# Stated order on ScalarE and VectorE from the router on, in an attention and two-layer mixture kernel on one core

## Chip, cores and metric

The kernel runs on one core of a Trainium2 chip. The metric is the device time of one execution in microseconds (us); the time before is the median of three runs.

## What is computed

The reference takes q, k, v (4 batches, 12 heads, 448 positions, head size 64), applies attention with a soft cap, and feeds the result (1792 tokens of 768 values) through a dense two-layer part and then through eight experts that are chosen greedily by logit, each with room for 224 tokens.

```python
x = _attn_ref(q, k, v, cap)
h = np.maximum(x @ w_in, 0.0); x = (h * h) @ w_out
logits = x @ w_gate
order = np.argsort(-logits.flatten())
...
out[mask] = np.maximum(x[mask] @ w1[e], 0.0) @ w2[e]
```

## The kernel before, in words

The work goes batch by batch (four batches of 448 tokens). `attention` and the dense part (`hidden`, `output`) of different batches are interleaved by `merge`. Most operands are split into a high and a low part, so that one product is three matmuls; the first layer of experts 0 to 3 is done in plain fp32 (`PLAIN`).

The change concerns what follows, `second` (line 137). It states, in one stream, the second layer of the dense part for the last two batches and then the experts (`experts`, line 179), and beside it the side streams: the logits, the eight routes (`route`, line 612) and their lists (`listed`, line 739). A planner clock `te` counts the TensorE time that has been stated; a side stream is taken up again when `te` has reached the time it asked for. The waits that side streams ask for are constants, for each of them one for the dense part and one for the experts: START (7.7, 8.0) from a route's preparation to its first mask matmul, MASK (1.85, 3.4), VOTE (1.0, 2.6), REST (0.86, 2.2), LIST (6.0, 10.0) from a list's operations to its matmul (L761).

A route finds the expert that fills up next, by six passes over digits of six bits: VectorE writes a mask (L640), TensorE multiplies it (L676), VectorE makes votes of that (L681 to L684), TensorE adds them up (L687), VectorE sets the digit (L690). Behind the passes come tm (L696), three small matmul steps, A and V (L716 to L719), the count matmul (L722), and then on VectorE, with no yield between them, sn, slot, n, room, base, fu, es, todo and ei (L723 to L735) and at once the next route's preparation: lim, L, m, sg, key, D0, digit, mask, eo, mx, B, need, di, dig (L618 to L665). The list of the route is a stream of its own that begins 0.5 later: off, half, rel, r, tk, oh (L747 to L757). The last route (number 7) has no passes.

An expert's first layer makes eight tiles of 128 features (L867 plain, L874 split) in PSUM tiles named acc, of which there are two; for expert 0, tiles 2 to 5 lie in tiles named big. `evict` empties one: ScalarE's Relu (L884), then VectorE's low part (L885), both under `high_priority(5000)`; the side streams run under `high_priority(2000)`. The second layer is L913. In its second half the next expert's rows are transposed (L802) through the same acc tiles and copied by ScalarE (L807, or L809 with VectorE's low part L810 from expert 4 on).

Expert weights are loaded by SyncE twelve tiles ahead (L834) and split four tiles ahead of use (`split_weights`: ScalarE's cast L361, VectorE's subtraction L362). A plain tile is not split.

What sets the order of the work: the framework compiles each engine's instructions into one in-order queue. Engines under `manual_schedule` keep stated order; the others are ordered at compile time by a simulated timeline and the priorities. Before the change only TensorE is manual. `issue_after(x)` puts an ordering edge behind x on x's own engine.

Of the kernel before, what the change touches and what calls it, by code (L numbers as in the profile page):

```python
# [16 lines left out]
OP = mybir.AluOpType  # L17
# [14 lines left out]
NF2 = F2 // 128  # L32
OB = 4
TC = N // 128
# [7 lines left out]
NS = 128  # L42
# [43 lines left out]
class Kernel:  # L86
# [5 lines left out]
    def run(self):  # L92
        tc = self.tc
        PS = bass.MemoryType.PSUM
        with tc.tile_pool(name="keep", bufs=1) as self.keep, \
                tc.tile_pool(name="wts", bufs=1) as self.wts, \
                tc.tile_pool(name="psum", bufs=2, space=PS) as self.psum, \
                tc.tile_pool(name="dram", bufs=1, space=bass.MemoryType.DRAM) as self.dram, \
                ExitStack() as right, ExitStack() as left:
            self.setup()  # L100
            self.mp = right.enter_context(tc.tile_pool(name="moe1", bufs=1, side="right"))
            self.gpool = self.mp
            xs = right.enter_context(ExitStack())
            self.xp = xs.enter_context(tc.tile_pool(name="x", bufs=ND, side="right"))
            with tc.tile_pool(name="x32", bufs=ND, side="right") as self.xq:
                with tc.tile_pool(name="rows", bufs=ND + 1, side="right") as self.tp, \
                        tc.tile_pool(name="attn", bufs=2, side="right") as self.ap:
                    merge([(self.attention(0), 44.0)])
                    self.split_rows(0)
                    merge([(self.hidden(0), 58.0), (self.attention(1), 44.0)])  # L110
                    for b in range(2, NB):
                        self.split_rows(b - 1)
                        streams = [(chain(self.output(b - 2), self.hidden(b - 1)), 118.0), (self.attention(b), 44.0)]
                        if b == NB - 1:
                            streams.append((self.gate_decode(), 30.0))
                        with tc.manual_schedule(engines={mybir.EngineType.PE}):
                            merge(streams)
                self.split_rows(NB - 1)
            self.gp = left.enter_context(tc.tile_pool(name="gate", bufs=1))
            last = left.enter_context(ExitStack())  # L120
            self.gpool = last.enter_context(tc.tile_pool(name="last", bufs=1))
            with tc.tile_pool(name="gate_load", bufs=3, side="right") as self.gl:
                with tc.manual_schedule(engines={mybir.EngineType.PE}):
                    merge([(self.hidden(NB - 1), 60.0), (self.gate_weights(), 80.0)])
            xs.close()
            self.tp = right.enter_context(tc.tile_pool(name="rows2", bufs=2, side="right"))
            self.rp = right.enter_context(tc.tile_pool(name="route", bufs=1, side="right"))
            self.router_setup()

            def room():  # L130
                last.close()
                self.ep = left.enter_context(tc.tile_pool(name="expert", bufs=2))

            with tc.manual_schedule(engines={mybir.EngineType.PE}):
                self.second(room)

    def second(self, room):
# [601 lines left out]
    def listed(self, k, es):  # L739

        nc, v = self.nc, self.nc.vector

        def T(shape, dt, name, bufs=1):
            return self.rp.tile(shape, dt, name=name, bufs=bufs)

        off, rel = T([128, 1], F32, "off"), T([128, TC], F32, "rel")
        v.tensor_scalar(off, es, float(CAP), float(CAP * NE + 1), op0=OP.mult, op1=OP.subtract)  # L747
        half, tk = T([128, TC, 2], BF, "half"), T([128, TC, 2, 2], BF, "tk")
        v.tensor_scalar(half[:, :, 0], self.slot, off, float(TP), op0=OP.add, op1=OP.is_lt)
        v.tensor_scalar(half[:, :, 1], self.slot, off, float(TP), op0=OP.add, op1=OP.is_ge)  # L750
        v.tensor_scalar(rel, self.slot, off, None, op0=OP.add)
        r = T([128, TC], BF, "r")
        v.scalar_tensor_tensor(r, half[:, :, 1], -float(TP), rel, op0=OP.mult, op1=OP.add)
        v.tensor_tensor(tk, self.tok[:, :, None, :].to_broadcast([128, TC, 2, 2]),
                        half[:, :, :, None].to_broadcast([128, TC, 2, 2]), op=OP.mult)
        oh = T([128, NS, TC], BF, "oh")
        self.picks = v.tensor_tensor(oh, self.slots, r[:, None, :].to_broadcast([128, NS, TC]), op=OP.is_equal)  # L757
        yield LIST[self.late], 0.0
        pi = self.psum.tile([128, 2, 2], F32, name="aux")
        for c in range(TC):  # L760
            nc.tensor.matmul(pi.rearrange("p a b -> p (a b)"), oh[:, :, c],  # L761
                             tk[:, c].rearrange("p a b -> p (a b)"), start=(c == 0), stop=(c == TC - 1))
        ix = T([TP, 2], F32, "ix")
        v.tensor_copy(ix, pi[:TP, :, 1])
        rows, idx = [], []
        for h in range(2):
            i = T([TP, 1], I32, f"idx{h}", 8)
            v.scalar_tensor_tensor(i, pi[:TP, h, 0:1], 128.0, ix[:, h:h + 1], op0=OP.mult, op1=OP.add)
            idx.append(i)
        while self.stored < DA or k > self.fed + 1 or k > self.gathered:  # L770
            yield 1.0, 0.0
        self.rows[k] = [self.gather(0, idx), None, idx]
        while self.stored < ND:
            yield 1.0, 0.0
        self.rows[k][1] = self.gather(1, idx)
        yield GATHER[k > 0], 0.8
        self.gathered = k + 1
# [65 lines left out]

    def split_expert(self):
        if len(self.ew[self.eready]) > 1:
            with self.tc.issue_after(self.picks.ins) if self.eready < 2 * NF2 else nullcontext():
                self.ew[self.eready] = self.split_weights(*self.ew[self.eready])

    def expert(self, k):
        nc, ep = self.nc, self.ep  # L850
# [83 lines left out]
def merge(streams):  # L934
    live = [[g, 0.0, total] for g, total in streams]
    while live:
        s = min(live, key=lambda x: x[1] / x[2])
        try:
            s[1] += next(s[0])
        except StopIteration:  # L940
            live.remove(s)
# [46 lines left out]
```

## Time and profile before

| | us |
|---|---|
| median of three runs (1072.57 to 1076.85) | 1075.96 |
| the profiled execution | 1073.57 |
| its span, first to last instruction | 1071.8 |
| PE busy | 1035.0 |
| DVE (VectorE) busy | 604.4 |
| ACT (ScalarE) busy | 470.8 |

The mean granted clock of TensorE is 0.991. The router's stage begins near 583 us, where the first matmuls of L562 stand, the first expert's matmuls near 749 us. Matmul records overlap, since they are pipelined; the step from start to start is what counts.

### The profile page before, as it was taken

Reading aid. Unit: us, or ns where it says so; the run is one execution under the profiler, and the core shown is the slowest. Engines: PE = TensorE matmul, PEld = TensorE weight load, DVE = VectorE, ACT = ScalarE, POOL = GpSimd, SP = SyncE. Lnnn points to the kernel's source line nnn. Section 1 sums busy time; section 2 is a strip of 40 time slices with the busy share of each in tenths; the row PEclk is TensorE's granted clock in tenths of the full one; section 3 lists DMA queues with packets and bytes.
Section 4 is the critical chain, followed back from the end, with each engine's and each line's share of the span. In section 5 each row is a group of like instructions: output and inputs, shape, how many; then the busy total and the mean of one; then the engine's idle time right before and its main releaser. Section 6 shows DMA issues by size and latency. Waiting matters only on the chain. (4 is left out here: it accounts for less than half of the span.)

```text
span 1071.8 us, 15662 instructions
## 1 busy us (share of the span) xinstructions
PE 1035.0 (97%) x5690; PEld 819.6 (76%) x5690; DVE 604.4 (56%) x1148; ACT 470.8 (44%) x725; POOL 245.8 (23%) x181
## 2 busy tenths in 40 slices
PE   6889999999999999999999999998999999999996
PEld 2235655777677777777887888887899998989996
DVE  5997999997222165556311244453656455676550
ACT  5867686544564633464543100012232232544551
POOL 0217785764221322221000100002220201021000
PEclk9999999999999999999999999998999999999999
DMA  8644777799655489978885368666673447556620
GB/s 284 240 149 139 253 274 255 243 323 339 228 176 185 164 293 343 367 274 283 294 297 173 126 195 283 194 203 199 209 273 144 134 164 274 187 189 208 212 72 27
DMA packets 102495, 237.60 MB, mean 222 GB/s; under 512 B 11089, under 2 KB 21873, under 8 KB 102417
## 3 DMA queue, kind: packets, MB, share of 16 engines
q1 hardware_dynamic: 87776, 219.65, 59.8%
q0 software_dynamic: 3424, 11.19, 3.4%
q10 hardware_dynamic: 11216, 5.75, 2.0%
q8 instruction: 45, 0.74, 0.3%
q14 instruction: 34, 0.27, 0.1%
HBM read 194.08 MB, written 42.47 MB: 221 GB/s over the span
## 5 line engine op out<-in xcount | busy, mean ns | idle before, releaser
L461 PE MATMUL acc<-g,wh 128*128 128x448 f32 x384 | 150.4, 392 | 0.0
L404 PE MATMUL acc<-xh,wh 128*128 128x448 f32 x384 | 146.4, 383 | 0.8 <-ACT r L411 0.8
L405 PE MATMUL acc<-xl,wh 128*128 128x448 f32 x384 | 140.7, 367 | 0.9 <-DVE xl L321 0.9
L462 PE MATMUL acc<-g,wh 128*128 128x448 f32 x384 | 140.9, 367 | 0.0
L463 PE MATMUL acc<-g,wl 128*128 128x448 f32 x384 | 140.3, 365 | 0.0
L406 PE MATMUL acc<-xh,wl 128*128 128x448 f32 x384 | 139.5, 363 | 0.0
L913 PE MATMUL big<-wh,g 128*112 128x384 f32 x512 | 119.3, 343 | 0.6 <-DVE g L885 0.6
L243 ACT ACTIVATE p<-big,isc 128x896 f32<-128x896 f32 x96 | 85.8, 907 | 43.5 <-PE big L239 43.5
L272 DVE RECIPROCAL z<-z 128x448 f32<-128x448 f32 x24 | 70.8, 2949 | 58.0 <-ACT z L271 58.0
L416 DVE TENSOR_TENSOR g<-r,g 128x448 fp32r<-128x448 f32 x58 | 42.7, 737 | 104.0 <-ACT g L415 103.7
L404 PEld LDWEIGHTS acc<-xh,wh 128*128 128x128 f32 x384 | 71.8, 188 | 34.7 <-issue 16.3
L783 POOL DMA_INDIRECT xg<-x,idx x32 | 31.5, 986 | 286.3 <-PE aux L676 129.4
L244 ACT ACTIVATE p<-p,capt 128x896 f32<-128x896 f32 x96 | 89.3, 948 | 1.7
L913 PEld LDWEIGHTS big<-wh,g 128*112 128x112 f32 x512 | 86.3, 176 | 1.6 <-DVE g L885 1.0
L461 PEld LDWEIGHTS acc<-g,wh 128*128 128x128 f32 x384 | 73.8, 192 | 11.8 <-issue 5.6
L263 PE MATMUL aux<-p,v 128*64 128x448 f32 x384 | 81.4, 550 | 0.3 <-DVE z L271 0.3
L239 PE MATMUL big<-qk 64*128 64x448 f32 x288 | 73.3, 599 | 7.1 <-DMA qk<-qk 6.4
L405 PEld LDWEIGHTS acc<-xl,wh 128*128 128x128 f32 x384 | 72.1, 188 | 10.4 <-issue 3.5
L361 ACT CAST wh<-wf 128x768 fp32r<-128x768 f32 (+1 forms) x64 | 47.9, 751 | 70.2 <-DMA wf<-w 13.9
L411 ACT ACTIVATE r<-acc 128x448 f32<-128x448 f32 x64 | 34.7, 543 | 99.1 <-PE acc L406 87.6
L462 PEld LDWEIGHTS acc<-g,wh 128*128 128x128 f32 x384 | 73.0, 190 | 6.3 <-issue 2.2
L463 PEld LDWEIGHTS acc<-g,wl 128*128 128x128 f32 x384 | 72.5, 189 | 6.8 <-issue 0.7
(179 smaller groups left out, 1838.2 us busy)
## 6 DMA issues: line engine op xcount, KB each, us to landing
g<-w SPq DMA_DIRECT2D x62, 384.0 KB
wh<-wih SPq DMA_DIRECT2D x48, 384.0 KB
wl<-wil SPq DMA_DIRECT2D x48, 384.0 KB
wh<-woh SPq DMA_DIRECT2D x72, 256.0 KB
wl<-wol SPq DMA_DIRECT2D x72, 256.0 KB
wf<-w SPq DMA_DIRECT2D x33, 384.0 KB
raw<-w SPq DMA_DIRECT2D x33, 384.0 KB
raw<-w_in SPq DMA_DIRECT2D x16, 768.0 KB
```

Source lines behind the costliest of these rows:

```text
L239: nc.tensor.matmul(ps[:, s, :S], k[rows], q[rows], start=True, stop=True)
L243: nc.scalar.activation(p, ps[:, :n, :S], AF.Tanh, scale=self.isc)
L244: e = nc.scalar.activation(p, p, AF.Exp, scale=self.capt)
L263: nc.tensor.matmul(U[hp][s * 64:s * 64 + 64], vt[hp][:, c, s * 64:s * 64 + 64], P[hp, c][:, s if c < KB else 0], start=(c == 0), stop=(c = ...
L272: nc.vector.reciprocal(d, d)
L404: nc.tensor.matmul(ps, wh[:, d], xh, start=(d == 0), stop=False)
L405: nc.tensor.matmul(ps, wh[:, d], xl, start=False, stop=False)
L406: nc.tensor.matmul(ps, wl[:, d], xh, start=False, stop=(d == ND - 1))
L461: nc.tensor.matmul(ps, a, gh, start=(f == 0), stop=False)
L462: nc.tensor.matmul(ps, a, gl, start=False, stop=False)
L463: nc.tensor.matmul(ps, z, gh, start=False, stop=(f == NF - 1))
L913: nc.tensor.matmul(acc[h][:, s, :DM // 2], l, r[:, s * (DM // 2):(s + 1) * (DM // 2)], start=(j == 0 and first), stop=(j == NF2 - 1 and last))
```

## The change

ScalarE and VectorE join TensorE in the manual schedule around `second`. The ordering edge that held the splits of the first expert behind the latest list's oh is dropped, and with it the attribute that named it.

```diff
-            with tc.manual_schedule(engines={mybir.EngineType.PE}):
+            with tc.manual_schedule(engines={mybir.EngineType.PE, mybir.EngineType.Activation, mybir.EngineType.DVE}):
                 self.second(room)
...
         oh = T([128, NS, TC], BF, "oh")
-        self.picks = v.tensor_tensor(oh, self.slots, r[:, None, :].to_broadcast([128, NS, TC]), op=OP.is_equal)
+        v.tensor_tensor(oh, self.slots, r[:, None, :].to_broadcast([128, NS, TC]), op=OP.is_equal)
...
     def split_expert(self):
         if len(self.ew[self.eready]) > 1:
-            with self.tc.issue_after(self.picks.ins) if self.eready < 2 * NF2 else nullcontext():
-                self.ew[self.eready] = self.split_weights(*self.ew[self.eready])
+            self.ew[self.eready] = self.split_weights(*self.ew[self.eready])
```

## Rows read from the trace of the kernel before

**Rows 1.** Waits of PE from 583 us: waited for, us in total, times, longest.
```profile
PE aux L687 <- DVE votes L684: 4.3, 3, 3.6
PE acc L867 <- DVE g L885: 2.4, 1, 2.4
PE acc L874 <- DVE g L885: 2.0, 4, 1.3
...
PE big L913 <- DVE g L885: 0.6, 2, 0.4
```

**Rows 2.** Two stretches: busy us of PE, PEld, DVE, ACT, POOL, then PEclk, DMA, GB/s.
```profile
742.20:749.10 6.90, 6.15 (x27) 5.32 (x27) 2.12 (x9) 2.35 (x4) 1.16 (x2) 0.51 0.00 1
...
885.60:889.00 3.40, 3.19 (x9) 2.91 (x10) 3.40 (x11) 1.12 (x3) 0.00 (x0) 0.50 0.02 8
```

**Rows 3.** Timelines of ACT and DVE near 740 us: start, us, what [idle before].
```profile
739.60 0.83 ACT L361 CAST wh<-g 128x768 fp32r<-128x768 f32 x1 [6.55 <-DMA g<-w]
...
740.47 0.96 DVE L362 TENSOR_TENSOR wl<-g,wh 128x768 fp32r<-128x768 f32 x1 [4.28 <-ACT wh L361]
```

**Rows 4.** Timeline of PE in the first layers of experts 5 and 7.
```profile
962.81 0.28 PE L874 MATMUL acc<-xs,wl 128*128 128x224 f32 x1
964.38 0.48 PE L874 MATMUL acc<-xs,wh 128*128 128x224 f32 x2 [1.29 <-DVE g L885]
...
1037.89 0.27 PE L874 MATMUL acc<-xs,wl 128*128 128x224 f32 x1
1038.27 0.48 PE L874 MATMUL acc<-xs,wh 128*128 128x224 f32 x2
```

**Rows 5.** Timeline of DVE around the end of route 1.
```profile
676.33 0.39 DVE L716 TENSOR_TENSOR A<-aux,room 128x224 bf16<-128x224 f32 x1 [1.10 <-PE aux L709]
...
677.67 0.39 DVE L726 TENSOR_REDUCE n<-aux 128x8 f32<-128x224 f32 x1
677.98 0.38 DVE L723 TENSOR_REDUCE sn<-V 128x14 f32<-128x224 f32 x1
...
680.85 1.07 DVE L757 TENSOR_TENSOR oh<-slots,r 128x1792 bf16<-128x1792 bf16 x1
...
683.33 0.26 DVE L636 TENSOR_TENSOR B<-eo,mx 128x112 bf16<-128x112 f32 x1
```

**Rows 6.** Timeline of DVE at the end of route 7.
```profile
964.24 0.38 DVE L726 TENSOR_REDUCE n<-aux 128x8 f32<-128x224 f32 x1
964.65 0.17 DVE L727 TENSOR_TENSOR room<-room,n 128x8 f32<-128x8 f32 x1
964.74 0.16 DVE L728 TENSOR_TENSOR base<-base,n 128x8 f32<-128x8 f32 x1
```

**Rows 7.** Timelines of DVE and PE: A of route 0, list matmuls of routes 0 and 1.
```profile
640.02 0.39 DVE L716 TENSOR_TENSOR A<-aux,room 128x224 bf16<-128x224 f32 x1 [0.46 <-PE aux L709]
...
648.48 0.66 PE L761 MATMUL aux<-tk,oh 128*128 128x4 bf16 x8
...
683.99 0.95 PE L761 MATMUL aux<-tk,oh 128*128 128x4 bf16 x14
```

**Rows 8.** Timelines of DVE and PE in the first layer of expert 0.
```profile
758.70 0.39 DVE L716 TENSOR_TENSOR A<-aux,room 128x224 bf16<-128x224 f32 x1 [2.15 <-issue]
...
766.87 2.43 PE L867 MATMUL acc<-xs,g 128*128 128x224 f32 x12
```

**Rows 9.** Timelines of DVE and PE in the first layer of expert 3.
```profile
876.91 0.39 DVE L885 SCALAR_TENSOR_TENSOR g<-acc,g 128x224 fp32r<-128x224 f32 x1 [1.09 <-ACT g L884]
...
880.97 2.43 PE L867 MATMUL acc<-xs,raw 128*128 128x224 f32 x12
```

**Rows 10.** Timeline of PE in the second layer of expert 4.
```profile
941.97 0.27 PE L722 MATMUL aux<-A,unit 128*128 128x224 bf16 x1
...
948.24 0.60 PE L802 MATMUL acc<-cf,xg 112*128 112x112 f32 x4
```

**Rows 11.** Instructions of L810: duration in ns min/median/max, first and last start.
```profile
L810 DVE TENSOR_TENSOR xs<-acc,xs x12: 615/618/625, 909.7 to 1024.9; 128x448 fp32r<-128x448 f32 x12
```

## The prediction

> **What bounds the kernel now.** I read the waits of TensorE first, over the stretch from the router on (583 us to the end) [rows 1]. TensorE waits for little there, and nearly all of it is for VectorE: votes that come late, and evictions (tile g, line 885) that come late. Every other engine matters only through those waits. Second, the clock [rows 2]: behind the two longest of them (3.6 and 2.4 us) the granted clock is 0.51 and 0.50, that is 1.2 instead of 2.4 GHz, once from 742.20 to 749.10 and once from 885.60 to 889.00; over matmuls that ran there the loss is about half: 3.1 and 1.6 us. Third, why the votes were late [rows 3]: the compile-time order had put a weight split ahead of them. ScalarE's cast waited 6.55 us for its load, VectorE's subtraction waited 4.28 us for that cast, and the router's three small operations stood behind it.
>
> So the stage's recoverable loss can be summed. Gaps: 4.1 (of the 4.3 for votes; one gap of 0.2 is of another kind), 2.4, 2.0 and 0.6 us, together 9.1 [rows 1]. A gap costs more than it shows: behind the 1.29 us one, start to start is 1.57 where 0.11 is the usual step, 0.17 on top [rows 4]; nine gaps give 1.5. Eight more are below that view's threshold, such as 0.38 where 0.11 is usual, 0.27 each [rows 4]: 2.2. With 4.7 for the clock it is **17.5 us**, the most the change can give back.
>
> **What the change does, part by part.**
>
> *TensorE's program* is in stated order already, and stays. *The release of the first expert's splits*: with VectorE in stated order a split is stated after the list it was held behind, so dropping the hold moves nothing: 0.
>
> *Splits go back to where they are stated*, four steps ahead of use, instead of wherever the compile-time schedule found room. The subtraction that delayed the votes is stated only when the fifth first-layer tile of expert 0 begins, behind those votes and the rest of that route's digits; its load, which landed for the cast at 739.60, is there by then. Evictions no longer meet a cast or a subtraction that ran further ahead. I take all 17.5 us as removed. Loads (SyncE) wait for buffers that these splits free, so they come later too; eight steps of about 2 us (18 matmuls of 0.11, [rows 4]) cover that, so 0; without the cover ScalarE would hold its evictions behind a load, as in [rows 3]. GpSimd's gathers follow the index operations and move by the list waits below; they feed a stage well after, so 0.
>
> *The router's bookkeeping becomes a block that nothing passes.* At each of the eight route ends the program states, in one go, the counts (10 operations), then the next route's limits, keys, first mask and choice (18), and one planner step later the list (7, the one-hot oh last). Now the order interleaves these three chains and lets evictions pass. In [rows 5] these 35 and one more (up) take 5.92 us (677.67 to 683.59), and oh ends at 681.92. In stated order most operations read what the one before them wrote. What that costs is in the rows: after n an operation that does not need it starts 0.31 later [rows 5], one that does 0.41 later, and behind room one that does not need it starts after 0.09 although room lasts 0.17 [rows 6]. So 0.10 for each of some 22 dependent neighbours, 2.3 us with the rounding: **8.2 us a block**, 0.5 for sn and slot and 7.7 from n to the end of oh. Bounds: 5.9, if the neighbours cost nothing, and 8.7 with a dependent step everywhere. I take 8.2, since these rows are of the same operations.
>
> Who waits for it?
>
> 1. *Lists of routes 0 to 2.* TensorE's matmul with oh is planned by the interleaved order. From A (676.33) the stated order needs 0.43, 0.19, 0.42 and 0.43 to sn and 0.5 to n, so n starts at 678.3 and oh ends at 686.0; the matmul came at 683.99 [rows 5, 7]: 2.1 us. Route 2 repeats this to 0.01; route 0 has A at 640.02 and the matmul at 648.48, so 1.3 [rows 7]. Sum 5.4. From route 3 on the planner puts 10 of its microseconds (LIST) between list and matmul instead of 6: 0.
>
> 2. *Route 3, in expert 0's first layer.* A starts at 758.70; V ends 1.4 later, one split (0.96, 0.87 to the next start) is stated next, so n starts at 761.4 and the block ends at 769.05. The first eviction is stated behind it, done at 769.45. TensorE's next tile on that PSUM buffer (two buffers of name acc) started at 766.87 [rows 8]: **2.7**.
>
> 3. *Route 5, in expert 3's first layer.* Eviction 0 at 876.91, sn, slot, n at 877.7, end 885.4. Eviction 1 waits for that, and tile 3 for it: it was under way at 880.97 [rows 9] and now starts at 885.85: **4.9**. The 2.40 us gap just behind in the old trace is among those removed.
>
> 4. *Route 6, in expert 4's second layer.* The next route is the last, with no digits, so 5.8 us from n at 942.45 (L722 at 941.97): 948.25. Then two splits and the subtraction of the first feed pair (0.62) [rows 10, 11] to 950.6; the third pair needs that pair's buffer at 948.24 [rows 10]: **2.4**.
>
> 5. *Route 7, in expert 5's first layer.* No next route: 3.8 us, but behind a split whose cast (0.83 [rows 3]) follows eviction 1 on ScalarE, so that it ends at 962.7. Eviction 2 is done at 966.9. Tile 2 ended at 962.9, or 962.5 once a 0.37 us wait ahead of it is gone; tile 3 takes 2.0, so tile 4, which needs that buffer, is ready at 964.5 [rows 4]: **2.4**.
>
> Route 4 ends in expert 1's second layer, with one split behind the block and 3 us of slack: 0. New waits: 5.4 + 2.7 + 4.9 + 2.4 + 2.4 = **17.8 us**.
>
> *Clock.* The old rows show a drop behind 3.55 and behind 2.40 us, none behind 1.29 [rows 1, 2, 4]. I charge the 4.9 like the longest (3.1), the 2.7 like the shorter (1.6), route 7's 2.4 (2.45 unrounded) also 1.6, and nothing for 2.35 and 2.1, which lie under the shortest that cost anything. Sum 6.3. Bounds: 0, and 3.1 + 5 x 1.6 = 11.1 if all but the first list's wait do it.
>
> **Sum:** -17.5 + 17.8 + 6.3 = +6.6 us. The profiled execution took 1073.57 us, 2.39 below the median of the three runs; carried over to the median 1075.96 the forecast is **1082.5 us**.
>
> **Rivals.**
>
> *The clock holds.* Same waits, no drop: -17.5 + 17.8 = +0.3, so 1076.3. For it: the waits are spread over 300 us, and three are close to the shortest that cost anything. Against: 2.40 did it [rows 2]. It decides at the wait of route 5.
>
> *The order inside a block costs nothing (faster).* The operations take 5.9 us in any order. Then the lists come in time (oh ends 683.7), route 3 costs 0.4, route 5 2.6, route 6 0.6, route 7 1.4, with one drop of 1.6: 6.6 - 17.5 = -10.9, so 1065. It decides at the two extra microseconds a block. Against it stand the two pairs of steps in [rows 5, 6]: 0.31 and 0.41 us behind the same operation. The Trainium skill, page "VectorE: DVE Perf Modes", section "The DRAIN you can't avoid", states this rule: an operation doesn't start until the pipeline of the one before has emptied, and semaphores between chained operations cost nothing extra. By that rule the sum is this rival's; the trace does not agree with it, since an independent operation starts 0.31 us after a 0.39 us one, before that has ended.
>
> *The clock falls behind nearly every new wait:* +0.3 + 11.1, so 1087.4.
>
> *The order does not change:* 1076. Against: the old order holds a subtraction ahead of votes that were stated long before it [rows 3]; TensorE's stated order is kept in a stage under the same manual schedule.
>
> **Chances.** Forecast 0.45, clock holds 0.27, order costs nothing 0.12, falls everywhere 0.12, nothing changes 0.04. 0.5% (5.4 us) is about what a measurement of this kernel can tell from no change. Slower by more: most of the forecast (its own range 1078 to 1087 begins below the line at 1081.4), 0.37, and the rival at 1087, 0.12: 0.49. Faster by more: 0.12, and 0.01 of the rest. Same: 0.38. The range leaves out the fast rival's centre at the bottom and reaches over the slow one's with 8.7 us blocks at the top: 1069 to 1090.
>
> **What would show it.** Right: no wait of TensorE for votes of several us; VectorE's route ends in stated order, sn before n and oh last, near 8 us; TensorE waiting for oh at three lists in the second layer of the dense part, and for g at route 3, 5 and 7, for xs at route 6; granted clock near 0.5 behind the wait of route 5. Wrong: blocks of 6 us, evictions inside the blocks, or ScalarE holding evictions behind a load.

## The result, and the profile after

The changed kernel took **1081.18 us** (median of 7 runs, 1079.33 to 1084.35) beside 1076.41 us for the kernel before on the same chip (7 runs): ratio **1.0052**, 95% interval 1.0036 to 1.0069. The forecast was 1082.5 us. On another chip, below, the changed kernel took 1083.23 us, but the kernel before only 1069.23, so there the ratio is 1.0132 (1.0103 to 1.0161). The change is a small loss on both, clear of the spread of the runs; its size depends on what the kernel before does on that chip.

The profiled execution of the changed kernel took 1083.09 us, the third longest of the seven; its span is 1081.3 us and its mean granted clock 0.984.

Waits of PE in the changed kernel from 583 us on, the view of [rows 1] (lines from 844 on have moved up by one: 884 is the eviction, 866 and 873 the first layers' matmuls):

```profile
PE acc L866 <- DVE g L884: 8.0, 3, 4.9
PE aux L761 <- DVE oh L757: 5.6, 3, 2.1
PE acc L873 <- DVE g L884: 2.3, 1, 2.3
PE acc L802 <- DVE xs L810: 2.1, 1, 2.1
...
PE aux L687 <- DVE votes L684: 0.2, 1, 0.2
```

Of the 4.3 us for votes 0.2 are left, and the old evictions' waits are gone. In their place stand the kinds that were forecast: oh at three lists, g in the first layers at routes 3 and 5 (both in the first row, with a third of 0.47 us) and 7, and xs at route 6.

VectorE's timeline at the end of route 1 in the changed kernel, to be read against [rows 5]:

```profile
680.96 0.39 DVE L723 TENSOR_REDUCE sn<-V 128x14 f32<-128x224 f32 x1
681.38 0.17 DVE L724 TENSOR_TENSOR slot<-slot,sn 128x14 f32<-128x14 f32 x1
681.47 0.38 DVE L726 TENSOR_REDUCE n<-aux 128x8 f32<-128x224 f32 x1
681.89 0.17 DVE L727 TENSOR_TENSOR room<-room,n 128x8 f32<-128x8 f32 x1
...
688.32 1.09 DVE L757 TENSOR_TENSOR oh<-slots,r 128x1792 bf16<-128x1792 bf16 x1
```

sn now stands before n and oh last. From n to the end of oh it is 689.41 - 681.47 = 7.94 us; 7.7 was forecast. What that does in an expert's first layer (route 5) shows on VectorE, with oh and the evictions behind it, and on PE:

```profile
890.71 1.08 DVE L757 TENSOR_TENSOR oh<-slots,r 128x1792 bf16<-128x1792 bf16 x1
891.71 0.68 DVE L884 SCALAR_TENSOR_TENSOR g<-acc,g 128x224 fp32r<-128x224 f32 x2
...
892.15 3.35 PE L866 MATMUL acc<-xs,raw 128*128 128x224 f32 x8 [4.86 <-DVE g L884]
```

Two evictions stand behind oh; PE has waited 4.86 us for the first of them.

The granted clock, in the view of [rows 2]: five stretches of the changed kernel, each behind one of its waits (the one from 889.90 began in the wait).

```profile
651.00:654.40 3.40, 3.40 (x16) 2.98 (x16) 0.47 (x4) 0.00 (x0) 0.00 (x0) 0.50 1.04 398
729.50:732.90 3.40, 3.40 (x16) 3.09 (x15) 0.46 (x4) 0.00 (x0) 2.11 (x3) 0.50 0.24 71
773.90:777.30 3.40, 3.40 (x11) 3.04 (x10) 2.18 (x6) 2.10 (x4) 0.00 (x0) 0.50 0.99 372
889.90:896.70 6.80, 4.55 (x12) 4.15 (x13) 2.42 (x9) 0.00 (x0) 0.00 (x0) 0.50 0.01 3
978.70:982.10 3.40, 3.40 (x19) 3.40 (x18) 1.53 (x3) 1.08 (x2) 0.00 (x0) 0.50 0.68 184
```

PEclk is the column with 0.50, that is 1.2 instead of 2.4 GHz. PE was busy 18.15 us in them (PE's column, the first after the comma, summed). By the prediction's rule half of that, 9.1 us, is what the half clock cost. This is an estimate, and a little high: behind the first list matmuls start 0.37 us apart (651.53, 651.91, 652.28) where the same ones start 0.20 apart at 2.4 GHz.

### The profile page after: what moved, and what is told of

Its sections match the earlier page's. It is cut to its first block, busy times and chain, and to the rows that moved or that the text cites. A ratio compares the mean times of both kernels' runs of the same rounds, so it can differ in the third digit from the quotient of the medians.

```text
span 1081.3 us, 15670 instructions
## 1 busy us (share of the span) xinstructions
PE 1037.6 (96%) x5690; PEld 822.7 (76%) x5690; DVE 619.0 (57%) x1148; ACT 467.1 (43%) x725; POOL 247.0 (23%) x181
## 4 chain that ended last, share of the span: by engine, by line
PE 75%; DVE 11%; issue 9%; ACT 2%; DMA 1%; POOL 1%; SPq 0%; POOLq 0%; DVEq 0%; ACTq 0%
PE big L912 8%; PE acc L461 7%; PE acc L404 7%; PE acc L462 7%; PE acc L463 7%; PE acc L405 6%; PE acc L406 6%; PE acc L866 6%; PE aux L263 5%; PE big L239 4%; PE acc L873 2%; PE aux L676 2%; PE aux L269 2%; PE big L241 2%; DVE wf L334 1%
## 5 line engine op out<-in xcount | busy, mean ns | idle before, releaser
L783 POOL DMA_INDIRECT xg<-x,idx x32 | 34.0, 1061 | 297.5 <-DVE ix L764 133.1
L406 PEld LDWEIGHTS acc<-xh,wl 128*128 128x128 f32 x384 | 72.3, 188 | 6.7 <-issue 0.8
```

Of the source, the lines that this page charges most:

```text
L406: nc.tensor.matmul(ps, wl[:, d], xh, start=False, stop=(d == ND - 1))
```

## The experiments

The theory is the prediction's: what the stated order removes is less than what the waits for VectorE's blocks, with the clock behind them, cost. The experiments take the two engines apart, then the block's places, its length and its wholeness, and last the hold.

**1. Each engine alone.** Two kernels that differ from the changed one only in the set of engines that keep the stated order:

```
-engines={mybir.EngineType.PE, mybir.EngineType.Activation, mybir.EngineType.DVE}
+engines={mybir.EngineType.PE, mybir.EngineType.DVE}            # VectorE alone
+engines={mybir.EngineType.PE, mybir.EngineType.Activation}     # ScalarE alone
```

VectorE alone. 

> Only VectorE (beside TensorE) keeps the stated order from the router on; ScalarE is ordered at compile time as before, and the hold is gone. VectorE's instructions stand in the changed kernel's order, to the last one; only ScalarE's differ. Theory (the blocks at the route ends on VectorE make the new waits): the same waits as in the changed kernel, lists 1.3, 2.1 and 2.1 us, route 3 2.7, route 5 4.9, route 6 2.1, route 7 2.3, and 1078 to 1085 us beside 1081 for the changed kernel. Rival (ScalarE's stated order, casts ahead of evictions, makes them): the evictions' waits at routes 3, 5 and 7 shrink to under 1 us each and the time falls to 1072 to 1075.

ScalarE alone. 

> Only ScalarE (beside TensorE) keeps the stated order; VectorE is ordered at compile time as before, the hold is gone. Theory (blocks on VectorE): no wait for oh at any list, since VectorE's chains interleave again; waits for votes and for g as in the kernel before, and a time near that, 1070 to 1080. Rival (ScalarE's stated order makes the new waits): waits for g of 2 us or more at routes 3, 5 and 7 and 1081 or more.

Measured, beside 1072.26 us for the kernel before: VectorE alone 1084.85 us (ratio 1.0111, 1.0083 to 1.0138), with the seven waits at their places (1.33, 2.13, 2.11, 2.56, 4.85, 2.35 and 2.46 us), so VectorE's order makes them, without ScalarE's. ScalarE alone **1055.32 us** (0.9841, 0.9815 to 0.9868): neither side had this, since the theory had expected the old waits for votes and g to stay. ScalarE's timeline there, in full, and one line of VectorE's show why the votes came in time:

```profile
731.96 0.58 ACT L441 COPY rows<-aux 112x512 f32<-112x512 f32 x1 [2.94 <-PE aux L439]
732.57 0.31 ACTq L442 DMA_DIRECT2D x<-rows  x1
739.41 0.53 ACT L807 COPY xs<-aux 128x448 f32<-128x448 f32 x1 [6.88 <-PE aux L802]
741.53 0.54 ACT L807 COPY xs<-aux 128x448 f32<-128x448 f32 x1 [1.58 <-PE aux L802]
742.76 0.53 ACT L480 COPY xt<-acc 128x448 f32<-128x448 f32 x1 [0.70 <-issue]
737.64 0.15 DVE L681 TENSOR_TENSOR left<-need,aux 64x8 f32<-64x8 f32 x1 [1.91 <-PE aux L676]
```

No weight cast stands between 731.96 and 742.76; in the kernel before one sat at 739.60 and made VectorE's subtraction, and behind it the votes, late [rows 3]. VectorE is ordered at compile time here; but with ScalarE's casts in their stated places, that order has no subtraction ahead of those votes: the first operation behind TensorE's mask matmul waits for that matmul (737.64) and not for a cast. Part of the 2.40 us gap near 885 us has the same cause: in the kernel before, a subtraction of 0.95 us at 884.50 stands between ScalarE's eviction (883.35) and VectorE's (885.37); with ScalarE alone VectorE has none in that layer until 876.25, behind the evictions of the first four tiles. The other late evictions were not followed one by one. VectorE's list chain is still interleaved: from n to the end of oh it is 4.25 us at routes 0 to 2, as in [rows 5].

Because the kernel before gave 1076 us on one chip and 1072 on the next, the four combinations were then run on a single chip, together with the last version below.

Both engines (the changed kernel). 

> The changed kernel itself, on one chip with the next three. Theory: 0.5 to 0.7% above the kernel before; the seven waits at the same places and of the same length to 0.1 us; the stretches at half clock behind the waits of 2.1 to 2.7 us partly at other places than in its first profile, since in the profiles so far about every second such wait has one. Rival on the clock (a given wait always has the same stretch behind it): stretches again behind route 0's list, route 2's list, route 3, 5 and 7, and none behind route 1's list and route 6.

VectorE alone. 

> VectorE alone in stated order, beside the changed kernel on one chip. If ScalarE's order works on its own whatever VectorE does, this lies 5 to 15 us above the changed kernel; if its gain was only in the waits that VectorE's stated order removes too (late votes), it lies within 3 us of it.

ScalarE alone. 

> ScalarE alone in stated order, on the same chip. From the sum of the prediction, the removed 17.5 us without the new waits and their clock (24.1): 17 us under the kernel before and 20 to 25 under the changed kernel.

| on one chip | median us | against before, 95% |
|---|---|---|
| before (neither) | 1069.23 | |
| ScalarE alone | 1054.18 | 0.9867 (0.9842 to 0.9892) |
| VectorE alone | 1083.03 | 1.0140 (1.0114 to 1.0167) |
| both (the change) | 1083.23 | 1.0132 (1.0103 to 1.0161) |

The ratio for both was expected at 1.005 to 1.007; it came out at 1.013, from a faster kernel before rather than a slower change. ScalarE's order gains 15 us where VectorE is free, and nothing (0.2 us) where VectorE is in stated order: what it removes, VectorE's order removes too. VectorE's order costs 29.05 us on top of ScalarE's; 20 to 25 were expected. ScalarE alone was expected 17 us under the kernel before and lies 15.05 under it. Waits of PE with ScalarE alone, all of them:

```profile
PE aux L802 <- DMA xg<-x,idx: 0.8, 1, 0.8
PE acc L866 <- ACT xs L807: 0.6, 1, 0.6
PE aux L676 <- DVE mask L640: 0.6, 1, 0.6
PE aux L687 <- DVE votes L684: 0.3, 2, 0.2
```

This is the stage without the old loss and without the new one: no wait of 1 us is left.

**2. The list later.** Only the planner's distance between list and matmul for routes 0 to 2:

```
-START, ..., LIST = (7.7, 8.0), ..., (6.0, 10.0)
+START, ..., LIST = (7.7, 8.0), ..., (9.0, 10.0)
```

> The changed kernel with 9 instead of 6 of the planner's microseconds between a list and its matmul for routes 0 to 2. Theory: the three waits for oh (1.34, 2.14, 2.12 us, 0.16 more each start to start) go, and the two stretches at half clock behind them (about 1.6 each) with them: 6 to 9.5 us less, 1071.5 to 1075.5. Rival (the waits are slack that another wait takes over, or the clock drops anyway): gain under 3 us, 1078 or more.

Measured 1072.35 us (ratio 1.0007, 0.9990 to 1.0023). The waits for oh are gone and the others stay:

```profile
PE acc L866 <- DVE g L884: 7.5, 2, 4.9
PE acc L873 <- DVE g L884: 2.2, 1, 2.2
PE acc L802 <- DVE xs L810: 2.1, 1, 2.1
```

The changed kernel took 1081.18 and 1083.23 us on two other chips, so some 9 to 11 us came from 5.6 us of waits; VectorE alone, as slow as the change on the chip of the table, took 1084.85 on this one, 12.5 us more. In the profile of this run no half clock is left between 583 us and the wait of route 5, so the clock behind the lists, which the prediction had left out, seems to have gone with them; route 3's wait, which stayed at 2.67 us, has none here either.

**3. The sequence inside a block.** The same 35 operations, restated so that the chains of counts, next route and list alternate (the sequence of the first six route ends; the first preparation and the last two route ends have shorter ones of their own):

```
 sn n slot room base lim fu lim2 fu2 L es m todo off sg half eo half2 key rel
 eo2 di D0 r mx di2 D tk mx2 oh dig mask B ei need
```

> The changed kernel with the same 35 operations at each route end stated in another sequence: the chains of the counts, of the next route and of the list alternate, so that few operations read what the one just before wrote. TensorE's and ScalarE's instructions stay as they are, and so do the evictions' places behind the blocks. Theory (a dependent neighbour costs 0.10 us, some 22 a block): the block takes about 5.9 instead of 7.9 us from n to its end; the lists' waits and route 6's go, route 3 falls from 2.7 to about 0.6, route 5 from 4.9 to about 2.7, route 7 from 2.3 to about 0.2; that is 14 to 15 us, and with most of the half-clock stretches gone 1057 to 1066. Rival (the sequence inside a block costs nothing, its length is the operations' own): blocks of 7.9 us and 1079 to 1084.

Measured 1061.68 us (0.9907, 0.9883 to 0.9931). VectorE at the end of route 1, in this kernel:

```profile
677.44 0.38 DVE L745 TENSOR_REDUCE n<-aux 128x8 f32<-128x224 f32 x1
677.74 0.17 DVE L744 TENSOR_TENSOR slot<-slot,sn 128x14 f32<-128x14 f32 x1
677.86 0.17 DVE L746 TENSOR_TENSOR room<-room,n 128x8 f32<-128x8 f32 x1
...
681.05 1.08 DVE L760 TENSOR_TENSOR oh<-slots,r 128x1792 bf16<-128x1792 bf16 x1
...
683.01 0.14 DVE L670 SCALAR_TENSOR_TENSOR need<-room,todo 64x8 f32<-64x8 f32 x1
```

From n to the block's end it is 683.15 - 677.44 = 5.71 us instead of 7.94, by sequence alone; slot starts 0.30 behind n, where room started 0.42 behind it in the changed kernel. Oh ends after 4.69, with five operations behind it. And the waits:

```profile
PE acc L887 <- DVE g L905: 3.0, 3, 2.4
PE acc L894 <- DVE g L905: 1.9, 1, 1.9
...
PE acc L823 <- DVE xs L831: 0.6, 1, 0.6
```

The lists wait no more, route 3 at most 0.2 us (0.6 expected), route 5 waits 2.44 (2.7 expected) and route 6 0.64 (0 expected). Route 7 stays at 1.92 (0.2 expected): it has no next route whose chain could alternate, and its evictions still stand behind all of it (the first 3.30 us behind n, 3.35 in the changed kernel). Behind none of these waits did the clock fall in the profile. The rival is out.

**4. The block in pieces.** The changed kernel, with two pauses (GAP is 2 of the planner's microseconds, START is shortened by as much), so that the list is stated before the next route and evictions can be stated in between:

```
         self.side.append([self.te + 0.5, self.listed(k, es)])
+        yield GAP[self.late], 0.0
...
             mask = compare(D)
+            if k:
+                yield GAP[self.late], 0.0
             choose()
```

> The changed kernel with each route end stated in three pieces, two of the planner's microseconds apart, instead of in one go: counts and list (17 operations, the list now before the next route's keys), then limits, keys and first mask, then the choice. The sequence inside a piece is as dependent as before, so the operations together take as long; evictions, feeds and splits can be stated between the pieces. Theory (it is the block's length ahead of oh and of the evictions that costs): oh ends some 4 us earlier, so no wait at the lists; the first eviction of route 3 and the second of route 5 pass after about 4.5 us of bookkeeping instead of 8, so about 0 and 1.5 us left; routes 6 and 7 under 1 us, or 7 unchanged at 2.3 since no next route stands behind it; 1056 to 1064. Rival (the dependent steps themselves are the cost, wherever they stand): 1072 or more.

Measured 1067.13 us (0.9970, 0.9954 to 0.9987), above the expected range and below the rival's 1072. The lists are in time, but:

```profile
PE acc L870 <- DVE g L888: 3.1, 3, 2.2
PE acc L877 <- DVE g L888: 2.2, 1, 2.2
PE acc L806 <- DVE xs L814: 2.1, 1, 2.1
```

Routes 6 and 7 are as they were (2.13 and 2.18 us). At route 5 VectorE's rows tell where the rest went:

```profile
872.52 1.08 DVE L761 TENSOR_TENSOR oh<-slots,r 128x1792 bf16<-128x1792 bf16 x1
873.52 0.38 DVE L888 SCALAR_TENSOR_TENSOR g<-acc,g 128x224 fp32r<-128x224 f32 x1
873.82 0.16 DVE L619 TENSOR_SCALAR lim<-room 128x8 f32<-128x8 f32 x1
...
878.29 0.68 DVE L888 SCALAR_TENSOR_TENSOR g<-acc,g 128x224 fp32r<-128x224 f32 x2
```

The first eviction now passes between list and next route (0.37 us of wait left), but the next two stand behind 4.5 us of the next route, and PE waits 2.23 us there. A pause only helps where an eviction happens to be stated in it.

**5. Both.** Alternating chains in three pieces.

> Both at once: chains alternate inside three pieces two planner's microseconds apart. If the two edits work on the same waits, as the theory has it, this lies at most a few us under the better of them: 1053 to 1060, the level of the kernel with ScalarE alone in stated order (1055.3), at which TensorE had no wait over 1 us. If VectorE's stated order itself cost something beside these waits, it would stay above 1060.

> Both engines in stated order, route ends in three pieces with alternating chains, on the same chip. Theory (VectorE's stated order costs nothing beside its waits): within 4 us of ScalarE alone. Rival (VectorE's stated order costs something of its own): 5 us or more above it.

Measured 1057.90 us (0.9882, 0.9854 to 0.9911), and 1057.39 us (0.9891) on the chip of the table, 3.2 us over ScalarE alone, inside the 4 expected. The longest wait from the router on is 0.84 us. So VectorE's stated order costs little by itself (3.2 us, more than the runs of either spread); the waits were most of its price. No version was found that beats ScalarE alone.

**6. The hold.** The kernel before, without it:

```
-            with self.tc.issue_after(self.picks.ins) if self.eready < 2 * NF2 else nullcontext():
-                self.ew[self.eready] = self.split_weights(*self.ew[self.eready])
+            self.ew[self.eready] = self.split_weights(*self.ew[self.eready])
```

> The kernel before, without the hold on the first expert's splits and nothing else: ScalarE and VectorE ordered at compile time. Theory (the hold is worth nothing, ScalarE's stated order alone gave the gain of the kernel in which it stands alone): the splits move ahead of the list, the votes wait as before or a little more, 1070 to 1080. Rival (dropping the hold gave that gain): 1052 to 1060.

Measured 1068.84 us (0.9987, 0.9966 to 1.0008). The hold is worth nothing that can be measured. Without it PE waits 4.76 us for votes at 738 us, where it was 3.55; but this wait also differs between two profiles of the kernel before, as the next run shows.

**7. The kernel before on another chip.**

> The kernel before itself, profiled on another chip, since its median was 1076 where the changed kernel was first timed and 1069 to 1072 on the three chips of the other runs, so that the ratio came out as 1.005 there and 1.013 later. Theory A (the late votes depend on when a load lands): ScalarE's cast near 740 us waits less than 6.55 us for its load, the wait for votes of 3.55 us is shorter by 2 us or more and the half clock behind it shorter or gone. Theory B (the clock alone): the same waits of TensorE to 0.3 us, fewer or shorter stretches at half clock. Theory C (neither): the same waits and stretches, and the time differs in the attention and dense part.

This chip gave 1076.55 us, like the first and unlike the three between, so the question of the 1069 us could not be put to it. It shows something else. Two lines of ScalarE's timeline, the first beside [rows 3]:

```profile
737.37 0.83 ACT L361 CAST wh<-g 128x768 fp32r<-128x768 f32 x1 [5.02 <-DMA g<-w]
778.24 0.83 ACT L361 CAST wh<-wf 128x768 fp32r<-128x768 f32 x1 [8.84 <-DMA wf<-w]
```

And the waits of PE, beside [rows 1]:

```profile
PE aux L687 <- DVE votes L684: 4.2, 3, 2.2
PE acc L874 <- DVE g L885: 3.9, 3, 3.3
PE acc L867 <- DVE g L885: 3.1, 2, 2.5
```

The first cast waited 5.02 us for its load instead of 6.55, and the longest wait for votes is 2.18 instead of 3.55, with 3.4 us at half clock behind it instead of 6.9: theory A, for that wait. But two others are longer, votes near 782 us (1.86 instead of 0.57) and one for g near 965 (3.34 instead of 1.29), and the time is the same. Ahead of the votes near 782 us too stands a subtraction whose cast had waited for its load (778.24). Ahead of the late g near 965 us the cast had waited 4.74 us for TensorE by the trace, not for a load, so that one stays unexplained. The waits of the kernel before thus differ between its two profiles, two of them with a load; those of the changed kernel do not: in its two profiles, on two chips, the seven agree to 0.1 us.

Why the kernel before takes 1069 to 1072 us on three of the five chips is open; no profile of it was taken there. The clock alone is not the reason: among its runs with a mean granted clock of 0.991, those on the chip of the table took 1069.34 and 1070.38 us, and those of this last chip 1075.17 or more.

## Why the prediction was right, and where it was off

**Removed, 17.5 us.** ScalarE alone has this term without the new waits: 15.0 and 16.9 us less than the kernel before on two chips, of a kernel before that took 1069 and 1072 us there. The term is right in size for those. The prediction did not ask which of the two engines removes it: either one's stated order does, so VectorE's was not needed for it.

**The block, 8.2 us, and 0.10 us for a dependent neighbour.** Measured 8.45 from sn to the end of oh, and from n on 7.94 against 5.71 us for the two sequences of the same operations: 2.2 us, where 2.3 was taken for 22 dependent neighbours. The rival *the order inside a block costs nothing* is out by experiment 3. The Trainium skill, page "VectorE: DVE Perf Modes", section "The DRAIN you can't avoid", was cited there for it: an operation doesn't start until the one before has emptied the pipeline. The trace of experiment 3 does not agree: slot starts 0.30 us into an n of 0.38. The same section adds, which the prediction did not say, that a next operation that is not held starts earlier; with that the trace agrees.

**New waits, 17.8 us.** The seven, forecast and measured:

| wait | forecast | measured |
|---|---|---|
| list of route 0 | 1.3 | 1.34 |
| lists of routes 1, 2 | 2.1, 2.1 | 2.14, 2.12 |
| route 3 | 2.7 | 2.69 |
| route 5 | 4.9 | 4.86 |
| route 6 | 2.4 | 2.14 |
| route 7 | 2.4 | 2.27 |
| route 4 | 0 | 0 |

Together 17.56 us. From the numbers that the prediction names, the lists come to 2.0, 2.0 and 1.2 and route 3 to 2.6, some 0.1 less each than it states; this changes nothing that follows. One wait of 0.47 at 847 us, in expert 2's first layer, was not foreseen; it is not in the second profile, and its cause is open.

**What was mis-sized.** Three terms, and that the time was hit all the same is partly luck.

First, a gap was charged 0.17 us more than it shows on the removed side, but not on the new one: the seven show 0.16 to 0.17 more from start to start, 1.2 us.

Second, the step "nothing for 2.35 and 2.1, which lie under the shortest that cost anything": in the first profile the half clock followed the lists' 1.34 and 2.12 us as well, and cost 9.1 us in all against 6.3. The sum of what was measured there, 17.56 + 0.47 + 1.2 + 9.1 = 28.3 us, fits that execution, which lies 27.8 and 28.9 us above ScalarE alone on two other chips. In the second profile, with four stretches, the same sum is 25.8 us, and that execution (1077.91 us) lies 23.7 above ScalarE alone on its chip, so the sum is good to some 2 us. The forecast had 24.1; between the medians on that chip lie 29.05. So the new side was some 2 to 5 us too cheap.

Third, the removed side. On the first chip ScalarE alone was not run; if it took 1054 to 1055 us there too, it lay 18 to 19 us under the execution that the 17.5 was read from (1073.57), but 21 to 22 under the median of the kernel before (1076.41). The prediction carried the 2.39 us between that execution and the median over to the changed kernel as it was. The waits of the kernel before differ between its profiles and those of the changed kernel do not, so this part of the median was most likely of the kind that the change removes. On the first chip this error and the two others cancelled. Where the kernel before had less to lose, the change cost 14.0 us (1083.23 - 1069.23), not 6.6.

**The rivals.** *The clock holds* (1076.3) is out: five stretches at half clock. *Falls behind nearly every new wait* (1087.4) is nearer than its chance said, five of seven in the first profile and four in the second, but 1.34 us was among them and two of 2.14 were not. *The order does not change* is out by VectorE's timeline of route 1.

## What to carry to other kernels

Where one engine feeds another (casts on ScalarE, subtractions on VectorE), fixing the stated order of the first can keep the second from running the wrong thing early. Here fixing both gained nothing more and gave up the compile-time order's interleaving. Before a stated order is kept, look for long runs of bookkeeping in it: alternate their chains so that neighbours don't depend on each other, and put what TensorE waits for ahead of what it does not. And time parts of a change one by one: here one part gained 15 us and the other lost 29 on top of it.

## What was not expected of the hardware

For waits of 1.3 to 2.7 us, their length does not tell whether the clock falls behind them. In ten profiles there are 47 waits of 1.2 us or more from the router on. All eight over 3 us have a stretch at half clock behind them; of 31 between 2.1 and 2.7 us 15 have one, and of eight under 2 us three. The place tells more: route 2's list (2.11 to 2.12 us) has it in 4 profiles of 4, route 7 (2.18 to 2.46) in 6 of 6, but route 1's list (2.13 to 2.14) in 1 of 4, route 6 (2.13 to 2.36) in 1 of 6 and route 3 (2.56 to 2.69) in 1 of 5. The second profile of the changed kernel shows both kinds:

```profile
727.50:730.90 3.40, 3.40 (x11) 3.02 (x10) 0.30 (x3) 0.00 (x0) 2.48 (x3) 0.50 0.41 112
773.00:776.40 3.40, 3.40 (x30) 3.17 (x29) 2.73 (x9) 2.30 (x5) 0.00 (x0) 1.00 1.02 405
```

The first lies behind 2.12 us (route 2's list) at 1.2 GHz, the second behind 2.67 us (route 3) at the full 2.4, where the first profile had 1.2. So the rival of that run, the same stretches each time, fails at route 3 and holds at the other six. What distinguishes the places was not tried. The changed kernel's runs spread over 6.7 us on that chip, those of ScalarE alone over 1.6. The waits kept their lengths in both profiles, and the mean granted clock goes with the time: 0.989 in the two shortest runs (1077.91 and 1079.04 us), 0.982 and 0.981 in the two longest (1084.10 and 1084.62). So the clock is the likely cause, though only one of these runs was profiled.
